# A linear-attention and mixture-of-experts kernel: loads one tile less ahead, two weight slices later, routing's matmuls and their readers issued apart

## The chip, the core and the metric

The kernel runs on one core of one Trainium2 chip. The metric is device time in microseconds of one execution, the median over several runs. Engines are named as the profile does: PE (TensorE, matmuls), DVE (VectorE), ACT (ScalarE), POOL (GpSimd), SP (SyncE, which here only issues DMAs).

## The reference

Two stages, the output of the first being the tokens of the second.

```python
for t in range(S):                       # B=4, H=8, S=768, D=48
    cur = einsum('bhd,bhe->bhde', u * k_t, v_t)
    y[:, :, t] = einsum('bhd,bhde->bhe', r_t, state + cur)
    state = w * state + einsum('bhd,bhe->bhde', k_t, v_t)
x = y as [3072 tokens, 384]
noisy = x @ w_gate + log1p(exp(x @ w_noise)) * noise     # 8 experts
top2 and their softmax weights per token
out[token] = sum over its 2 experts of weight * (relu(x @ w1[e]) @ w2[e])   # 384 -> 1024 -> 384
```

## The kernel before

**Attention** is done in 24 tiles of 128 rows (4 batches, 6 chunks; loop from L1224). Per tile: POOL forms kd (k times a table of decay, L391) and rku (r times k times u, L398 and L402); PE turns kd and r to head-major (KX and RV, L217); ACT and DVE evict them as kT and rT (L428, L430); PE forms the scores PAB (L443), DVE masks them as am (L451, two halves); PE forms py (L499), DVE adds the u term: x (L518), which SP stores to the DRAM tensor xd. Then PE turns x and multiplies it by the gate weights (L527), ACT copies the logits lg (L536). The work of neighbouring tiles overlaps: turn and scores of tile i+1 are issued in iteration i.

**Loads.** `load(i, part)` (L143) issues k, r and v of a tile on SP, in the row with everything else that SP issues: x stores, the noise nz, slices of expert 0's weights (stg, L338). In iteration i, k and r of tile i+6 and v of tile i+5 are issued; the prologue has loaded tiles 0 to 4 and k, r of 5. `W_LD` (L47) says in which iteration each of the seven weight slices is loaded, `W_AT0` (L48) from which iteration on its split into a high and a low part runs (ACT L344, L347, DVE L346, L349).

**Routing** runs beside attention, by groups of eight tiles (tiles 0 to 7, 8 to 15, 16 to 23). `route(g)` (L674) is a generator that issues one or two small DVE instructions between yields: the noisy logits, the two largest, softmax weights GTS, the count of earlier tokens per expert by matmuls into RT (L763 to L766, read by acc L767 and SLF L772), and the list of expert 0's rows. That list is made by `drop` (L627): one-hot tables r_oa and r_ob on DVE, then `place` (L653), which issues eight matmuls (L656) and in the same call DVE's reader of them (L660 or L662). `place` is put on the list `late_mm` and called two ticks later. In attention, `one_step` (L1131) advances a route by one yield, eight times per tile; `tick` (L1121) calls what is due in `late_mm`. In the expert stage `rstep` (L1159) does both, with a credit per call.

**Experts.** Each expert takes up to 832 rows, in chunks of tiles of 128: `p1(e, ci)` is the first matmul (ph L1044, evicted by ACT L1046 and DVE L1048 to hb), `p2(e, ci)` the second (pym L1078, 24 per tile of rows). Rows of a chunk come by a gather on POOL (xg, L947) that takes its indices from GR (DVE L810 to L812, after `place`), and PE turns them (ptm, L970). Expert 0's chunk 0 needs only group 0's tokens, its chunk 1 group 1's, and chunk 2 the rest. Gather and turn of chunk 1: `list_01` (L1197) gathers when group 1's `place` has run; the turn is issued at the fourth and fifth call of `step` in p2(0,0) (L1312), eight pym matmuls each. Chunk 2's are at the fourth to sixth call in p2(0,1) (L1346). While p1(0,0) runs, SP issues sixteen stores of zeros to the output (`zero_out`, L1212).

Of the kernel before, what the change touches and what calls it, by code (L numbers as in the profile page):

```python
# [43 lines left out]
W_AT = ((3, 7, 8), (3, 5, 7, 9))  # L44
NOT = 4

W_LD = {1: 0, 3: 1, 5: 2, 7: 3, 9: 4, 11: 5, 14: 6}  # L47
W_AT0 = (4, 6, 8, 11, 13, 16, 18)  # L48


@with_exitstack
def kernel(
# [574 lines left out]
    def drop(g, mm2, ej2, ijv, w_, c0, first):  # L627

        i0, i1 = GROUPS[g]
        n = i1 - i0  # L630
        wp_ = w_ + w_ % 2
        T = T_of(n)
        oa = T("oa", [128, n, 128], BF16, 2)
        ob = T("ob", [128, n, 2 * E * NJ], BF16, 2)[:, :, :2 * wp_].rearrange("p n (a b) -> p n a b", a=2)
        sh = [128, n, 64, 2]
        nc.vector.tensor_tensor(oa.rearrange("p n (a b) -> p n a b", b=2), mm2[:, :, None, :].to_broadcast(sh),  # L636
                                im[:, None].to_broadcast(sh), op=ALU.is_equal)
        yield 0.6
        c = 0.1 + 0.005 * wp_
        sh = [128, n, wp_ // 2, 2]  # L640
        o0, o1 = (ob[:, :, a].rearrange("p n (a b) -> p n a b", b=2) for a in range(2))
        nc.vector.tensor_tensor(o1, ej2[:, :, None, :].to_broadcast(sh),
                                ijv.rearrange("p (a b) -> p a b", b=2)[:, None].to_broadcast(sh), op=ALU.is_equal)
        yield c
        nc.vector.tensor_mul(o0, o1, thi[:, i0:i1, None, :].to_broadcast(sh))
        yield c
        late_mm.append([2, lambda: place(n, oa, ob, wp_, w_, c0, first),
                        lambda: nc.scalar.activation(ob[:, :, 1], ob[:, :, 1], AF.Copy, scale=pcol)])
        yield 0.05

    late_mm = []

    def place(n, oa, ob, wp_, w_, c0, first):  # L653
        pL = RT[:, 6 * GB * E:6 * GB * E + 2 * wp_].rearrange("p (a b) -> p a b", a=2)
        for j in range(n):
            nc.tensor.matmul(pL.rearrange("p a b -> p (a b)"), oa[:, j, :],  # L656
                             ob[:, j].rearrange("p a b -> p (a b)"), start=(j == 0), stop=(j == n - 1))
        Lv = L[:, :, c0:c0 + w_]
        if first:
            nc.vector.tensor_copy(Lv, pL[:, :, :w_])  # L660
        else:
            nc.vector.tensor_add(Lv, Lv, pL[:, :, :w_])  # L662
# [11 lines left out]
    def route(g, lists=True):  # L674
# [8 lines left out]
        if g:  # L683
            while lists and late_mm and g < len(GROUPS) - 1:
                yield "hold"
            pc = RT[:, 5 * GB * E:5 * GB * E + E]
            nc.tensor.matmul(pc, ones_b, acc, start=True, stop=True)
            sh0 = T("da", [128, n])[:, 0:1]
            nc.vector.tensor_scalar(sh0, pc[:, 0:1], -1.0, float(EARLY[g]), op0=ALU.mult, op1=ALU.add)
            yield  # L690
            nc.vector.tensor_max(ie_n[:, 0, 0:1], ie_n[:, 0, 0:1], sh0)
# [72 lines left out]
        for j in range(1, n):  # L764
            nc.tensor.matmul(pr[:, j:], ones_b, om[:, :n - j], start=False, stop=False, skip_group_check=True)
        nc.tensor.matmul(pr, ones_b, acc[:, None, :].to_broadcast(sh), start=False, stop=True, skip_group_check=True)  # L766
        nc.vector.tensor_add(acc, acc, sm[:, :, 0])  # L767
        next(ex, None)
        yield
# [351 lines left out]
    def tick():  # L1121
        for x in late_mm:
            x[0] -= 1
            if x[0] == 1:
                x[2]()
        while late_mm and late_mm[0][0] <= 0:
            late_mm.pop(0)[1]()
            credit[0] -= 0.25
        at_pe[0] = max(at_pe[0] - 1, 0)

    def one_step():  # L1131
        k = 0
        while len(route_q) > k and not at_pe[0]:
            try:
                c = next(route_q[k])
            except StopIteration:
                route_q.pop(k)
                continue
            if c == "wait" and k == 0 and FILL:
                k = 1  # L1140
                continue
            if c == "pe":
                at_pe[0] = 2
            return

    consts_a()
# [3 lines left out]
    uterm_u(0)  # L1150
    scores(0)
    mask(0)
    load(4)
    load(5, (0, 2))
    warm(WARM3)
    turn_kr(1)
    uterm_b(0)
# [1 line left out]
    def rstep(us, lag=2):  # L1159

        credit[0] = min(credit[0] + us, 1.6 * us + 0.2)
        for x in late_mm:
            x[0] -= 1
            if x[0] == 1:
                x[2]()
        while late_mm and late_mm[0][0] <= 0:
            late_mm.pop(0)[1]()
            credit[0] -= 0.25
        k = 0
        while len(route_q) > k:  # L1170
            if at_pe[0] > 0:
                at_pe[0] -= 1
                if at_pe[0] > 0:
                    return
            if credit[0] <= 0:
                return
            try:
                c = next(route_q[k])
            except StopIteration:
                route_q.pop(k)  # L1180
                continue
            if c == "wait" and k == 0 and FILL:
                k = 1
                continue
            if c in ("hold", "wait"):
                return
            if c == "pe":
                at_pe[0] = lag
                credit[0] -= 0.3
                return  # L1190
            credit[0] -= c or 0.25
# [31 lines left out]
    flag = consts_c()  # L1223
    for i in range(NT):  # L1224
        products(i)
        if i + 6 < NT:
            load(i + 6, (0, 2))
        if i == I_EARLY:
            while 0 not in routed or late_mm:
                rstep(1)  # L1230
            early(0)
        if i in (4, 6):
            next(flag)
        if 1 <= i <= B:
            load_nz(i - 1)
        if i == B:
            consts_b()
        if i:
            kvup(i)
        yout(i)  # L1240
        if not i:
            kvup(i)
        if i + 5 < NT:
            load(i + 5, (2, 3))
        zup_v(i)
        if i:
            zblock(i - 1)
            uterm_c(i, CV_EARLY, H)
            logits_out(i - 1)
            route_when_done(i - 1)  # L1250
        tick()
        one_step()
        one_step()
        if i + 1 < NT:
            uterm_b(i + 1)
        one_step()
        one_step()
        xout(i)
        one_step()
        if i == NT - 1:  # L1260
            xT_first()
            turn_x(i)
            p1a = p1(0, 0)
        else:
            turn_kr(i + 2)
            uterm_c(i + 1, 0, CV_EARLY)
            scores(i + 1)
            turn_x(i)
            mask(i + 1)
            tick()  # L1270
            one_step()
        if not i:
            consts_v()
        for p, t in enumerate(W_AT0):
            if W_LD.get(i) == p or t <= i <= t + 2:
                next(wun[p])
# [264 lines left out]
```

## Time and profile before

| | us |
|---|---|
| median of 3 runs (lowest, highest) | 591.69 (591.44, 592.29) |
| profiled execution | 594.2 |
| its span | 592.5 |
| attention, to the first matmul of p1(0,0) | 133.3 |
| p1(0,0), to the first pym of p2(0,0) | 143.12 |
| PE busy | 565.8 (96%) |
| DVE busy | 359.4 (61%) |
| ACT busy | 286.5 (48%) |
| POOL busy | 274.0 (46%) |

The shares are of the whole span. A window's row gives the busy time of each engine in a stretch, the number of instructions after an x, then the granted clock of PE as a share of full speed, the busy share of the DMA engines and GB/s. A row of waits says who waited for what: total, times, longest. In a timeline, the bracket at the end of a row is the idle time of its engine before it, and what ended it.

### The profile page before, as it was taken

How to read it: one execution, taken by the hardware profiler on the slowest of the kernel's cores; microseconds unless marked ns; L12 is line 12 of the kernel's file. 1: busy time of each engine (PE TensorE's matmuls, PEld its weight loads, DVE VectorE, ACT ScalarE, POOL GpSimd, SP SyncE). 2: the span in 40 equal slices, each digit the busy share in tenths (PEclk: the TensorE clock that was granted, in tenths of full speed). 3: DMA queues.
4: the chain of work that ended last, by engine and by line, in shares of the span. 5: the costliest groups of instructions: out<-in, count | busy, mean ns of one | idle time of the engine just before them, and what ended most of it. 6: DMA issues, size and time to landing. Idle time of an engine off the chain costs nothing.

```text
span 592.5 us, 13758 instructions
## 1 busy us (share of the span) xinstructions
PE 565.8 (96%) x5281; PEld 540.4 (91%) x5282; DVE 359.4 (61%) x866; ACT 286.5 (48%) x721; POOL 274.0 (46%) x420
## 2 busy tenths in 40 slices
PE   7897987889999999999999999999999999999995
PEld 5897886879999999999999999999999999999995
DVE  5998998977886554546455645555454546454331
ACT  4456786853362633554445554454545454445220
POOL 8987876721015543426333552344242526333222
PEclk9899999999999999999999999999999999999999
DMA  9989999429514643874655645464845555423211
GB/s 149 192 204 191 225 209 196 102 70 267 182 60 146 203 143 84 194 173 152 140 168 113 198 114 175 102 181 111 198 129 159 153 134 174 124 93 84 66 35 42
DMA packets 143016, 86.44 MB, mean 146 GB/s; under 512 B 118415, under 2 KB 133006, under 8 KB 142944
## 3 DMA queue, kind: packets, MB, share of 16 engines
q1 hardware_dynamic: 132384, 56.67, 40.6%
q0 software_dynamic: 9936, 28.83, 15.9%
q8 instruction: 43, 0.70, 0.5%
q14 instruction: 29, 0.24, 0.1%
q10 hardware_dynamic: 624, 0.00, 0.1%
HBM read 58.83 MB, written 19.76 MB: 133 GB/s over the span
## 4 chain that ended last, share of the span: by engine, by line
PE 79%; DVE 10%; DMA 5%; ACT 2%; POOL 2%; issue 2%; POOLq 0%; SPq 0%; ACTq 0%
PE ph L1044 35%; PE pym L1078 33%; PE py L499 2%; PE pym L1069 2%; PE pym L1071 2%; DVE am L451 2%; DMA stg<-in_moe_w_dram 2%; DVE x L518 2%; DVE rT L430 1%; DMA xg<-xd,GR 1%; DMA out_dram<-ot,TK 1%; PE KX L217 1%; DVE c L410 1%; PE py L527 1%; PE PAB L443 1%
## 5 line engine op out<-in xcount | busy, mean ns | idle before, releaser
L1078 PE MATMUL pym<-w1h,hb 128*128 128x384 f32 x768 | 200.6, 337 | 0.0
L1048 DVE SCALAR_TENSOR_TENSOR hb<-ph,hb 128x384 fp32r<-128x384 f32 (+1 forms) x136 | 72.5, 533 | 116.3 <-ACT ht L1046 68.4
L1044 PE MATMUL ph<-xh,w0h 128*128 128x384 f32 (+3 forms) x408 | 140.0, 344 | 0.0
L1078 PEld LDWEIGHTS pym<-w1h,hb 128*128 128x128 f32 x768 | 139.4, 188 | 0.3
L1044 PE MATMUL ph<-xh,w0l 128*128 128x384 f32 (+3 forms) x408 | 138.8, 341 | 0.0
L1044 PE MATMUL ph<-xl,w0h 128*128 128x384 f32 (+3 forms) x408 | 133.5, 341 | 0.0
L1078 PE MATMUL pym<-w1l,hb 128*128 128x384 f32 x384 | 129.5, 337 | 0.0
L1046 ACT ACTIVATE hb<-ph 128x384 fp32r<-128x384 f32 (+1 forms) x136 | 64.2, 472 | 107.7 <-PE ph L1044 105.0
L1101 POOL DMA_INDIRECT out_dram<-ot,TK x56 | 58.8, 1050 | 103.6 <-DVE ot L1097 52.6
L947 POOL DMA_INDIRECT xg<-xd,GR x56 | 61.2, 1092 | 70.6 <-DVE r_oa L636 18.8
L1044 PEld LDWEIGHTS ph<-xh,w0h 128*128 128x128 f32 x408 | 76.7, 188 | 3.3 <-ACT xh L987 0.2
L1044 PEld LDWEIGHTS ph<-xh,w0l 128*128 128x128 f32 x408 | 76.7, 188 | 2.6
L1044 PEld LDWEIGHTS ph<-xl,w0h 128*128 128x128 f32 x408 | 76.1, 188 | 2.8
L1078 PEld LDWEIGHTS pym<-w1l,hb 128*128 128x128 f32 x384 | 72.1, 188 | 0.1
L956 POOL DMA_INDIRECT pv<-out_dram,GA x49 | 49.8, 1016 | 48.2 <-DMA out_dram<-ot,TK 35.8
L1018 ACT ACTIVATE xh<-xj 128x384 fp32r<-128x384 f32 (+1 forms) x42 | 21.1, 502 | 43.5 <-DVE xj L1016 41.6
L1086 ACT ACTIVATE ot<-pym 128x384 f32<-128x384 f32 x39 | 19.0, 486 | 40.6 <-PE pym L1078 29.9
L1019 DVE TENSOR_TENSOR xl<-xj,xh 128x384 fp32r<-128x384 f32 (+1 forms) x42 | 22.4, 534 | 24.7 <-ACT xh L1018 13.6
L1004 ACT ACTIVATE pl<-xg 128x768 uint16<-128x768 uint16 (+1 forms) x42 | 35.3, 841 | 1.0 <-DMA xd<-pl 0.9
L391 POOL TENSOR_TENSOR kd<-kt,tabk 128x192 f32<-128x192 f32 x46 | 27.7, 624 | 12.8 <-PE RV L463 6.4
L451 DVE TENSOR_TENSOR am<-PAB,mneg 128x512 int32<-128x512 int32 x48 | 31.6, 680 | 1.9 <-PE PAB L443 1.8
L419 ACT ACTIVATE cv<-vt,c 128x48 f32<-128x48 f32 x120 | 30.2, 323 | 5.0 <-DVE c L410 2.6
(272 smaller groups left out, 827.3 us busy)
## 6 DMA issues: line engine op xcount, KB each, us to landing
stg<-in_moe_w_dram SPq DMA_DIRECT2D x24, 512.0 KB
stg<-in_moe_w_dram SPq DMA_DIRECT2D x32, 384.0 KB
rd<-in_r_dram SPq DMA_DIRECT2D x24, 192.0 KB
vt<-in_v_dram SPq DMA_DIRECT2D x24, 192.0 KB
xd<-x SPq DMA_DIRECT2D x24, 192.0 KB
out_dram<-ot SPq DMA_DIRECT2D x16, 288.0 KB
kt<-in_k_dram SPq DMA_DIRECT2D x23, 192.0 KB
xg<-xd,GR POOLq DMA_INDIRECT x56
```

Source lines behind the costliest of these rows:

```text
L391: nc.gpsimd.tensor_mul(KD[i][:, h], kt[i][:, h], tabk[:, h, :D])
L419: nc.scalar.activation(CV[i][:, h, :], vt[i][:, h, :], AF.Copy, scale=C8[i][:, h, :])
L451: nc.vector.tensor_tensor(am[:, :, h].bitcast(I32), pa[:, :, h].bitcast(I32), mneg[:, None].to_broadcast([128, 2, NP // 2, 128]), op=ALU.b ...
L947: nc.gpsimd.indirect_dma_start(out=xg[:n], out_offset=None, in_=xd[:rows_of(early_)], in_offset=bass.IndirectOffsetOnAxis(ap=GR[:n, e * NJ ...
L956: nc.gpsimd.indirect_dma_start(out=pv[:n], out_offset=None, in_=out, in_offset=bass.IndirectOffsetOnAxis(ap=GA[:n, e * NJ + t:e * NJ + t + ...
L1004: nc.scalar.activation(pl[:n], XG[e, t][:n, :DM].bitcast(U16).rearrange("p (d two) -> p two d", two=2), AF.Copy)
L1019: nc.vector.tensor_sub(xl, xj, xh.bitcast(F32))
L1044: nc.tensor.matmul(ph[:, :w_], a[:, d, fs], x[:, d, :w_], start=(j == 0), stop=(j == len(q) - 1))
L1046: nc.scalar.activation(h_[:, f, 0, :], ph[:, a:b], AF.Relu)
L1048: nc.vector.scalar_tensor_tensor(h_[:, f, 1, :], ph[:, a:b], 0.0, h_[:, f, 0, :].bitcast(F32), op0=ALU.max, op1=ALU.subtract)
L1078: nc.tensor.matmul(py, hb[:, f, a, hs], x[:, f, :], start=(j == 0), stop=(j == len(q) - 1))
L1101: st = nc.gpsimd.indirect_dma_start(out=out, out_offset=bass.IndirectOffsetOnAxis(ap=TK[:n, q:q + 1], axis=0), in_=ot[:n], in_offset=None, ...
```

## The change

Loads: the prologue leaves out v of tile 4 and k, r of tile 5; iteration i loads k and r of tile i+5 and v of tile i+4. Weight slices 5 and 6 are loaded in iterations 14 and 17 instead of 11 and 14, and the splits of slices 3 to 6 begin in iterations 10, 12, 17 and 20 instead of 11, 13, 16 and 18. `place` is split: the matmuls are issued at one tick and the reader (`placed`) at the next one. In `route`, two yields stand between a matmul and its reader. One `one_step` call less stands in each tile.

```diff
-W_LD = {1: 0, 3: 1, 5: 2, 7: 3, 9: 4, 11: 5, 14: 6}
-W_AT0 = (4, 6, 8, 11, 13, 16, 18)
+W_LD = {1: 0, 3: 1, 5: 2, 7: 3, 9: 4, 14: 5, 17: 6}
+W_AT0 = (4, 6, 8, 10, 12, 17, 20)
...
-        late_mm.append([2, lambda: place(n, oa, ob, wp_, w_, c0, first),
-                        lambda: nc.scalar.activation(ob[:, :, 1], ob[:, :, 1], AF.Copy, scale=pcol)])
+        pL = RT[:, 6 * GB * E:6 * GB * E + 2 * wp_].rearrange("p (a b) -> p a b", a=2)
+        late_mm.append([2, lambda: place(n, oa, ob, pL),
+                        lambda: nc.scalar.activation(ob[:, :, 1], ob[:, :, 1], AF.Copy, scale=pcol),
+                        lambda: placed(pL, w_, c0, first), False])
...
-    def place(n, oa, ob, wp_, w_, c0, first):
-        pL = RT[:, 6 * GB * E:6 * GB * E + 2 * wp_].rearrange("p (a b) -> p a b", a=2)
+    def place(n, oa, ob, pL):
...
+
+    def placed(pL, w_, c0, first):
...
             nc.tensor.matmul(pc, ones_b, acc, start=True, stop=True)
+            yield "pe1"
...
         nc.tensor.matmul(pr, ones_b, acc[:, None, :].to_broadcast(sh), start=False, stop=True, skip_group_check=True)
+        yield "pe1"
         nc.vector.tensor_add(acc, acc, sm[:, :, 0])
...
-        while late_mm and late_mm[0][0] <= 0:
-            late_mm.pop(0)[1]()
-            credit[0] -= 0.25
+        if late_mm and late_mm[0][4]:
+            late_mm.pop(0)[3]()
+        if late_mm and late_mm[0][0] <= 0:
+            late_mm[0][1]()
+            late_mm[0][4] = True
...
-            if c == "pe":
-                at_pe[0] = 2
+            if c in ("pe", "pe1"):
+                at_pe[0] = 2 if c == "pe" else 1
...
-    load(4)
-    load(5, (0, 2))
+    load(4, (0, 2))
...
         while late_mm and late_mm[0][0] <= 0:
-            late_mm.pop(0)[1]()
+            x = late_mm.pop(0)
+            if not x[4]:
+                x[1]()
+            x[3]()
             credit[0] -= 0.25
...
+            if c == "pe1":
+                continue
...
-        if i + 6 < NT:
-            load(i + 6, (0, 2))
+        if i + 5 < NT:
+            load(i + 5, (0, 2))
...
-        if i + 5 < NT:
-            load(i + 5, (2, 3))
+        if i + 4 < NT:
+            load(i + 4, (2, 3))
...
         one_step()
         if i + 1 < NT:
             uterm_b(i + 1)
-        one_step()
         one_step()
```

Three places show how it moves the instructions. The first is DVE in attention around the reader acc of group 0's counting matmuls (zt is the state update, c the u term's sum, r_sm the counts, w1l the low part of a weight slice). Before:

```order
L410 TENSOR_REDUCE c_1811<-rku 128x8
L518 TENSOR_TENSOR x<-py,cv 128x384
L430 TENSOR_TENSOR rT<-RV,pwr 128x2x4x64
L451 TENSOR_TENSOR am<-PAB,mneg 128x2x256 x2
L349 TENSOR_TENSOR w1l_1129<-stg,w1h_1128 128x384
L476 TENSOR_TENSOR zt<-RV,z_210 128x192
L767 TENSOR_TENSOR acc<-acc,r_sm 128x8
L558 TENSOR_SCALAR RT<-r2r 128x8
L772 TENSOR_TENSOR SLF_239<-RT,ie_n 128x64
L561 SCALAR_TENSOR_TENSOR RT<-RT,r2r 128x8
L410 TENSOR_REDUCE c_1936<-rku 128x8
```

And now:

```order
L476 TENSOR_TENSOR zt<-RV,z_210 128x192
L410 TENSOR_REDUCE c_1927<-rku 128x8
L518 TENSOR_TENSOR x<-py,cv 128x384
L430 TENSOR_TENSOR rT<-RV,pwr 128x2x4x64
L451 TENSOR_TENSOR am<-PAB,mneg 128x2x256 x2
L772 TENSOR_TENSOR acc<-acc,r_sm 128x8
L558 TENSOR_SCALAR RT<-r2r 128x8
L349 TENSOR_TENSOR w1l_1124<-stg,w1h_1123 128x384
L476 TENSOR_TENSOR zt<-RV,z_211 128x192
L777 TENSOR_TENSOR SLF_239<-RT,ie_n 128x64
L561 SCALAR_TENSOR_TENSOR RT<-RT,r2r 128x8 x2
L410 TENSOR_REDUCE c_2045<-rku 128x8
```

The matmuls that acc reads stand on PE after its py of the same tile. The reader stood behind the state update zt of its tile; now the x addition, the rT eviction and both masks of the next tile stand between, and SLF comes two more instructions later. L767 has become L772, L772 is L777.

The second is DVE at the rows GR of expert 0's chunk 1, from which the gather of p2(0,0) takes its indices (hb is the eviction of p1, PS the route of group 2, xl<-ptm the reader of the turned rows). Before, the reader of ptm stood 22 rows further down:

```order
L693 SCALAR_TENSOR_TENSOR PS<-lg 128x64
L695 TENSOR_SCALAR r_a<-PS 128x64
L696 SCALAR_TENSOR_TENSOR PS<-lg,nz 128x64
L549 TENSOR_SCALAR PS<-r_a 128x64
L1048 SCALAR_TENSOR_TENSOR hb<-ph,hb 128x256
L662 TENSOR_TENSOR L<-L,RT 128x2x7
L810 SCALAR_TENSOR_TENSOR lt<-L 128x2
L811 TENSOR_SCALAR lt<-lt 128x2
L812 TENSOR_SCALAR GR<-lt 128x2
L1048 SCALAR_TENSOR_TENSOR hb<-ph,hb 128x256
L551 TENSOR_SCALAR PS<-PS 128x64
```

And now:

```order
L558 TENSOR_SCALAR PS<-r1r 128x64
L561 SCALAR_TENSOR_TENSOR PS<-PS,r1r 128x64 x2
L665 TENSOR_TENSOR L<-L,RT 128x2x7
L815 SCALAR_TENSOR_TENSOR lt<-L 128x2
L816 TENSOR_SCALAR lt<-lt 128x2
L817 TENSOR_SCALAR GR<-lt 128x2
L561 SCALAR_TENSOR_TENSOR PS<-PS,r1r 128x64 x2
L977 TENSOR_TENSOR xl<-ptm,xh 128x3x128
L561 SCALAR_TENSOR_TENSOR PS<-PS,r1r 128x64
L563 SCALAR_TENSOR_TENSOR PS<-PS,r1s 128x64
```

GR is computed within p2(0,0), after all of p1(0,0)'s evictions, and the reader of ptm is two rows behind it. On PE, the eight matmuls of `place` (L657) stand behind 24 pym of p2(0,0), and ptm 8 pym behind them; before, they stood in p1(0,0) and 32 pym of p2(0,0) lay between p1's end and ptm. In p2(0,1) it is the same with 16 pym before `place` and 16 behind it; there `place` stood ahead of the first pym.

The third is SP at the end of attention (r_a are the gate weights of a group that are stored beside x, out_dram<-ot the zero stores). Before:

```order
L520 DMA xd<-x 128x384
L152 DMA vt<-in_v_dram 128x8x48
L520 DMA xd<-x 128x384 x6
L793 DMA xd<-r_a 128x8x8
L1213 DMA out_dram<-ot 192x1x384 x16
L793 DMA xd<-r_a 128x8x8
L338 DMA stg<-in_moe_w_dram 128x1024 x3
```

And now:

```order
L152 DMA vt<-in_v_dram 128x8x48
L520 DMA xd<-x 128x384
L152 DMA vt<-in_v_dram 128x8x48
L520 DMA xd<-x 128x384 x5
L1224 DMA out_dram<-ot 192x1x384 x10
L798 DMA xd<-r_a 128x8x8
L1224 DMA out_dram<-ot 192x1x384 x6
L798 DMA xd<-r_a 128x8x8
```

Group 1's gate weights, which the gather of chunk 1 reads with the rows, stand behind ten of the zero stores; before, ahead of all.

## Rows read from the trace of the kernel before

**Rows 1.** The page, busy us (share of the span) and instructions.

```profile
PE 565.8 (96%) x5281; PEld 540.4 (91%) x5282; DVE 359.4 (61%) x866; ACT 286.5 (48%) x721; POOL 274.0 (46%) x420
```

**Rows 2.** Windows of 10 us (us, busy of each engine, PEclk, DMA, GB/s).

```profile
100.00:110.00 10.00, 7.82 (x191) 7.13 (x192) 9.65 (x31) 6.93 (x22) 5.79 (x12) 1.00 0.92 198
140.00:150.00 10.00, 10.00 (x74) 9.92 (x74) 8.41 (x40) 2.73 (x8) 1.93 (x2) 1.00 0.95 296
```

**Rows 3.** Window, the tiles from x9 to x23.

```profile
58.13:132.29 74.16, 62.27 (x1521) 57.25 (x1523) 68.00 (x205) 53.98 (x185) 50.13 (x87) 0.98 0.71 163
```

**Rows 4.** Waits of DVE, 50 to 134 us.

```profile
DVE acc L767 <- PE RT L766: 2.8, 2, 2.2
...
DVE L L660 <- PE RT L656: 1.4, 1, 1.4
```

**Rows 5.** Timeline of DVE, first and last of group 1's moved part.

```profile
120.67 0.16 DVE L747 TENSOR_SCALAR r_da<-r_da 128x8 f32<-128x8 f32 x1
...
132.77 0.21 DVE L792 TENSOR_TENSOR r_a<-r_os 128x64 f32<-128x64 f32 x1
```

**Rows 6.** Timeline of PE, tile 22: py of the masked scores.

```profile
126.06 1.09 PE L499 MATMUL py<-vt,am 128*64 128x48 f32 x32
```

**Rows 7.** Timeline of DVE: acc of group 1, x22.

```profile
127.52 0.17 DVE L767 TENSOR_TENSOR acc<-acc,r_sm 128x8 bf16<-128x8 bf16 x1 [2.24 <-PE RT L766]
...
128.89 0.55 DVE L518 TENSOR_TENSOR x<-py,cv 128x384 f32<-128x384 f32 x1
```

**Rows 8.** Waits of ACT (25:80) and POOL (10:80) for loads.

```profile
ACT w0h L344 <- DMA stg<-in_moe_w_dram: 4.6, 2, 3.0
...
POOL kd L391 <- DMA kt<-in_k_dram: 5.2, 5, 1.8
```

**Rows 9.** Timeline of SP: weight slice 2.

```profile
50.63 1.42 SPq L338 DMA_DIRECT2D stg<-in_moe_w_dram  x1
```

**Rows 10.** Windows, all engines, around the idle PE at 56 us.

```profile
55.97:58.80 2.83, 0.00 (x0) 0.00 (x0) 1.38 (x8) 2.79 (x12) 2.14 (x5) 0.93 1.23 226
58.80:61.80 3.00, 2.91 (x46) 2.75 (x48) 3.00 (x8) 2.70 (x10) 2.60 (x6) 0.50 0.83 188
```

**Rows 11.** Timeline of PE: p2(0,0) start, ptm; p2(0,1) start, place.

```profile
143.12 0.34 PE L1078 MATMUL pym<-w1h,hb 128*128 128x384 f32 x1
...
148.76 0.49 PE L970 MATMUL ptm<-ident,xg 128*128 128x128 f32 x3
...
161.33 0.42 PE L1078 MATMUL pym<-w1h,hb 128*128 128x384 f32 x1
...
165.65 0.53 PE L656 MATMUL RT<-r_ob,r_oa 128*128 128x100 bf16 x8
```

**Rows 12.** Timeline of DVE: GR of chunk 1; chunk 2.

```profile
142.27 0.17 DVE L812 TENSOR_SCALAR GR<-lt 128x2 int32<-128x2 f32 x1
...
161.79 0.42 DVE L1048 SCALAR_TENSOR_TENSOR hb<-ph,hb 128x256 fp32r<-128x256 f32 x1
162.12 0.16 DVE L662 TENSOR_TENSOR L<-L,RT 128x14 f32<-128x14 f32 x1
...
162.72 0.17 DVE L812 TENSOR_SCALAR GR<-lt 128x3 int32<-128x3 f32 x1
162.79 0.68 DVE L636 TENSOR_TENSOR r_oa<-r_dm,im 128x1024 bf16<-128x1024 bf16 x1
```

**Rows 13.** Timeline of POOL: gathers of chunk 1 and of chunk 2.

```profile
142.71 0.98 POOL L947 DMA_INDIRECT xg<-xd,GR  x1 [15.77 <-DVE GR L812]
144.00 0.95 POOL L947 DMA_INDIRECT xg<-xd,GR  x1 [0.30 <-issue]
163.74 0.95 POOL L947 DMA_INDIRECT xg<-xd,GR  x1 [18.79 <-DVE r_oa L636]
```

**Rows 14.** DMA, gathers' queue: 142.5 to 146.0, 163.5 to 166.5.

```profile
q0 software_dynamic: 64, 0.20, 26.0%
...
q0 software_dynamic: 64, 0.20, 26.3%
```

## The prediction

> **What bounds the kernel now.** I read the page's engine totals first, then windows, then the waits of one engine at a time. The totals [rows 1] say that TensorE (PE) is busy for 96% of the span and VectorE (DVE) for 61%, but that is an average over two stages. The windows separate them [rows 2]: from 140 us on PE is busy 10.0 of 10 us at full clock, so the expert stage costs what PE has to do, and anything PE waits for there is added whole. In the attention stage it is the other way round: from 100 to 110 us DVE is busy 9.65 of 10 and PE 7.82. So in attention a DVE instruction or a DVE stall that goes is worth its time, until another engine's chain ends later; in the expert stage small DVE instructions are free. I cut the attention loop at the starts of its x additions, one per tile: from the tenth to the last tile (x9 to x23) it is 74.16 us, of which DVE works 68.00 and is idle 6.16 [rows 3].
>
> Times of the sum are those of the profiled execution (594.2 us, span 592.5). The median of the runs shown is 591.69; I add the differences to the median, since what the sum changes is a difference. A difference of 0.2% (1.2 us) is about what a measurement of this kernel can tell from none.
>
> **Readers issued apart, and eight steps per tile to seven.** The waits of DVE [rows 4] are what the split removes: 2.8 us before acc L767, which reads RT behind nine matmuls, and 1.4 before L660, which reads place's matmuls. The order shows in place of these waits a mask (am) or another tile's work between matmul and reader. The step that is missing per tile makes routing later: the part of group 1 from L747 to L792, 23 small instructions of 0.16 to 0.29 us, leaves the attention loop and is done in the expert stage's first p1. The first and the last are in [rows 5]; together they are 4.05 us. If DVE alone set the end, 4.05 + 2.8 + 1.4 = 8.25 us would go. It does not quite, and I go through the places:
> - Eight of the 23 stand before acc, in tiles where DVE has nothing idle: 1.43 us, all gained.
> - Tile 22, where 2.24 of the acc wait is: x22 starts at 128.89 [rows 7]. Without acc before it, it still needs PE's py, which ends at 126.06 + 1.09 = 127.15 [rows 6]. So 1.74 goes, not 2.24 and the instructions behind it.
> - The other acc wait, 2.8 - 2.24 = 0.6, and L660's 1.4: both gained, 2.0.
> - Of tile 23, behind x22, I take 0.4 for the instructions that leave it, since PE's chain there is hardly shorter than DVE's, and 0.2 for L792 [rows 5], which stands ahead of the first expert's xl.
> That is 1.43 + 1.74 + 2.0 + 0.4 + 0.2 = **5.8 us** gained, with ends 3.5 (x22 and x23 wait for ACT or PE just as long) and 8.25. What the moved instructions cost in the expert stage is nothing by themselves: in 140 to 150 us DVE is busy 8.41 of 10 [rows 2], and PE waits for none of it but what the next part says.
>
> **Loads one tile later, weights 5 and 6 later.** SyncE's queue issues transfer after transfer in the attention loop, each waiting its turn, so a transfer's place in the row decides when it starts. With one k/r/v triple less ahead of it, each slice of weights starts earlier. Slice 2 was issued at 50.63 [rows 9] and ACT waited 2.98 us for it, to 55.52; over both slices 4.6 us [rows 8]. With it comes an idle PE from 55.97 to 58.80 with the clock at 0.50 in the 3.0 us behind it [rows 10]. So a gain of up to the length of that idle time, 2.8 us, is there. Against it, POOL already waits 5.2 us in five places for k [rows 8], and k of tile n is now issued one iteration later, behind one more x store and in part one more slice: k itself comes some 1.5 us later, and POOL's product kd is ahead of the turn and scores of the next tile. So one wait is exchanged for another in the same tiles. I take **0.6 us** gained, ends 2.8 gained and 2.5 lost (half of the 5.2 again). Slices 5 and 6 have their splits in tiles 17 to 22 instead of 16 to 20; they are needed in the first p2 alone (143 us), so nothing waits. The DVE halves of the split are the same count.
>
> The Trainium skill (DMA: Bandwidth & Descriptors, Rules for kernel authors) speaks against this part: to overlap transfer and work, issue the DMA early and wait late. By that rule the 0.6 gained would be the 2.5 lost. The trace does not show it settled, since the row of transfers is full either way: what is issued early there is late for another.
>
> **The first two gathers of the expert stage.** This is the part that costs. Group 1's place matmuls now stand inside p2(0,0), behind 24 of its pym matmuls, where they stood in p1(0,0), before. Call T the start of p2(0,0); it was 143.12, and the first turn ptm came at 148.76 = T + 5.64, 32 matmuls of 0.176 us later [rows 11]. Before, the rows GR were computed at 142.27 [rows 12], ahead of T, the gather ran from 142.71 [rows 13], its 64 packets were done by 146.0 [rows 14], and PE waited for nothing. Now: 24 matmuls x 0.176 = T + 4.2, place 0.3, then L665 and L815 to L817, 0.8 us as from 162.12 to the end of GR at 162.89 [rows 12]: T + 5.35. The gather starts 0.3 us behind GR's end: T + 5.6. It lands 3.3 us later under the zero stores (142.71 to 146.0), 2.8 without them (163.74 to 166.5) [rows 13, 14]: T + 8.4 to 8.9. PE is at ptm at T + 5.64 + 0.25 for the added matmuls, T + 5.9. PE's wait is **2.8 us**, ends 2.3 and 4.1 (the chunk's second gather, issued 1.3 us behind the first [rows 13], is waited for whole).
>
> In p2(0,1) the same happens to group 2. PE reaches its first ptm 32 pym and eight place matmuls (0.35) after the start, T2 + 5.9 ([rows 11] has T2 = 161.33 and the place at 165.65). DVE has a chain of twelve instructions, two of them r_oa of 0.68 us [rows 12], the others 0.16 to 0.2, after the last hb of p1(0,1), which ended at 161.79 + 0.42, T2 + 0.9: then T2 + 4.3, GR at T2 + 5.0, gather T2 + 5.3, landed T2 + 8.1. PE waits **2.2 us**, ends 1.0 and 2.75. The gathers of the third chunk have a whole p1 more and are not waited for.
>
> Behind an idle time of 2.83 us PE's granted clock was 0.50 for 3.0 us [rows 10], the 1.2 GHz level. Of two waits of 2.8 and 2.2 us I let one be followed by that: 3.0 x 0.5 = **1.5 us**, ends 0 and 3.0.
>
> **Sum:** -5.8 - 0.6 + 2.8 + 2.2 + 1.5 = +0.1. Rounded to what this bears, 591.5 us: no change, with a gain in attention paid back in the first two p2.
>
> **The rivals.**
> 1. *The weights come in time and no wait for k takes their place* (chance 0.24). The idle PE at 56 us is gone, its whole 2.83 us with it. For it: the longest single wait of that stretch is the one for a slice. Against: five k waits. With 2.8 in place of 0.6, and no clock fall in p2: 591.5 - 2.2 - 1.5 = 587.8.
> 2. *Loads issued later are late* (0.16). Place: POOL's kd in tiles 5 to 12. It decides if k of a tile lands more than about 1 us later than now, for there the turn of the tile has no slack. 2.5 lost in place of 0.6 gained: 591.5 + 3.1 = 594.6, slower. It is the case that the rule in the Trainium skill (DMA: Bandwidth & Descriptors, Rules for kernel authors) would bring.
> 3. *More waiting in the expert stage* (0.10): the second gather of the chunk is waited for too, with the upper ends 4.1 and 2.75, and both clock falls: 591.5 + 1.3 + 0.55 + 1.5 = 594.9, slower.
> 4. *The gathers are covered after all* (0.08), because DVE and the gather are quicker than I price them: without 2.8 + 2.2 + 1.5 the time is 585.0. The order speaks against it: in DVE's row the reader of ptm stands two rows behind GR.
>
> **How the numbers follow.** My forecast has 0.42, its own range 589.8 to 593.2: 0.08 of it over 1.2 us faster, 0.28 within, 0.06 slower. Faster: 0.08 + 0.22 of rival 1 + 0.08 of rival 4 = 0.38. Same: 0.28 + 0.02 of rival 1 = 0.30. Slower: 0.06 + 0.16 + 0.10 = 0.32. For 8 in 10 the range takes in rivals 1 and 2 and most of 3, and leaves 4 out: 587.0 to 595.4.
>
> **What would show it.** In the profile after, DVE should have no wait for RT at acc L772 and L663 and x9 to x23 should be some 68 us; expert work should start near 127 us instead of 133.3. The ACT wait for stg should be under 1 us, POOL's for kt should be 5 us or more. PE should be idle 2 to 4.5 us before the first ptm of p2(0,0) and 1 to 2.75 before that of p2(0,1), released by the DMA xg, with a granted clock of 0.50 behind at least one. If PE is idle in neither, the main costs are wrong and the time is rival 4's; if the expert stage starts later than 130 us, the attention gain is wrong.

## The result, and the profile after

The changed kernel takes 600.57 us (median of 4 runs, 598.14 to 602.03) against 591.99 us (591.44 to 594.12). The ratio over all the runs is 1.0134, with a 95% interval of 1.0086 to 1.0182; the quotient of the two medians is 1.0145. It is slower, outside the range of the prediction. The ratios of this document leave out executions more than 1.5% above the fastest of their kernel, which are three of e10's five (606.7 to 609.5 us, the traced one among them). Its profiled execution, the shortest of the four, took 598.14 us with a span of 596.4. Rows below are of that execution; their differences to the rows of before therefore add up to 3.9 us, not to the 8.6 between the medians.

The attention loop did what was expected, and more. One window, from x9 to x23 as in [rows 3]:

```profile
57.00:123.99 66.99, 59.89 (x1512) 55.81 (x1514) 64.49 (x186) 53.94 (x184) 50.02 (x87) 1.00 0.79 178
```

74.16 us have become 66.99, and p1(0,0) starts at 125.03 in place of 133.33. DVE works 64.49 us in place of 68.00. The waits of DVE (50 to 134 us, the largest three), to be held against [rows 4], and the waits of POOL for k (10 to 80 us), against [rows 8]:

```profile
DVE hb L1053 <- ACT hb L1051: 2.9, 3, 1.6
DVE x L518 <- ACT lg L536: 1.0, 2, 0.8
DVE zt L476 <- PE RV L463: 0.3, 1, 0.3
```

```profile
POOL kd L391 <- DMA kt<-in_k_dram: 7.9, 7, 2.5
```

No wait for RT is left on DVE. ACT has no wait for a weight slice there; POOL waits 7.9 us for k where it waited 5.2.

All of it and more is paid back in the expert stage. The timeline of PE at the start of p2(0,0), at its `place` matmuls, at its first ptm, and at the start and the first ptm of p2(0,1), against [rows 11]:

```profile
134.75 0.34 PE L1083 MATMUL pym<-w1h,hb 128*128 128x384 f32 x1
...
139.10 0.36 PE L657 MATMUL RT<-r_ob,r_oa 128*128 128x16 bf16 x8
...
144.64 0.90 PE L975 MATMUL ptm<-ident,xg 128*128 128x128 f32 x3 [3.67 <-DMA xg<-xd,GR]
...
158.58 0.34 PE L1083 MATMUL pym<-w1h,hb 128*128 128x384 f32 x1
...
167.83 0.60 PE L975 MATMUL ptm<-ident,xg 128*128 128x128 f32 x3 [3.15 <-DMA xg<-xd,GR]
```

Two idle times of 3.67 and 3.15 us, each ended by the DMA of a gather. Behind both the granted clock falls to the 1.2 GHz level; two windows of PE's work from the end of each idle time (the number before DMA share and GB/s is the clock):

```profile
144.64:148.10 3.46, 3.46 (x15) 3.42 (x15) 1.86 (x6) 0.58 (x2) 0.00 (x0) 0.57 0.09 36
167.83:171.30 3.47, 3.47 (x19) 3.42 (x20) 1.95 (x7) 1.10 (x3) 0.29 (x1) 0.54 0.21 71
```

A mean of 0.57 and 0.54 over 3.5 us: in both places nearly the whole stretch is at half clock, as in [rows 10]. Summed over half-microsecond windows, 3.4 us are lost to the clock, 0.2 of them while PE is still idle.

Why the first gather is so late is seen on DVE, POOL and SP. DVE from the writing of r_a over the instruction that waits to GR, and GR of chunk 2; POOL's gathers; SP's zero stores (the first two answer to [rows 12] and [rows 13]):

```profile
134.16 0.23 DVE L797 TENSOR_TENSOR r_a<-r_os 128x64 f32<-128x64 f32 x1
...
138.25 0.20 DVE L699 TENSOR_SCALAR r_a<-PS 128x64 f32<-128x64 f32 x1 [0.92 <-DMA xd<-r_a]
...
140.23 0.16 DVE L665 TENSOR_TENSOR L<-L,RT 128x14 f32<-128x14 f32 x1
...
140.82 0.17 DVE L817 TENSOR_SCALAR GR<-lt 128x2 int32<-128x2 f32 x1
...
163.53 0.17 DVE L817 TENSOR_SCALAR GR<-lt 128x3 int32<-128x3 f32 x1
```

```profile
141.26 0.98 POOL L952 DMA_INDIRECT xg<-xd,GR  x1 [22.00 <-DVE PS L561]
142.55 0.95 POOL L952 DMA_INDIRECT xg<-xd,GR  x1 [0.30 <-issue]
164.55 1.11 POOL L952 DMA_INDIRECT xg<-xd,GR  x1 [21.06 <-DVE r_ob L645]
```

```profile
124.96 8.91 SPq L1224 DMA_DIRECT2D out_dram<-ot  x10
134.41 0.49 SPq L798 DMA_DIRECT2D xd<-r_a  x1
134.95 5.69 SPq L1224 DMA_DIRECT2D out_dram<-ot  x6
```

The store of group 1's r_a stands behind ten zero stores in SP's row, but what it waited for is r_a itself: L797 ended at 134.39, and SP issued the store at 134.41. It landed 3.7 us later, where the two other stores of r_a in this execution took 2.4 and 2.9 us. So r_a was still being read when group 2's route wanted to write the tile again: DVE waits 0.92 us at L699, and L665, three rows of DVE ahead of GR, has to wait with it. What L665 reads, the `place` matmuls, had ended at 139.46, and L665 starts at 140.23; without the wait for r_a it could have started at most 0.8 us earlier. The gather starts at 141.26, T + 6.5 with T = 134.75, and PE gets on at T + 9.9.

The same stretches in all the executions traced, in us. The first column of times ends at the start of x9, the second goes from x9 to x23, and the ratio is the one to before on the same chip, with its 95% interval; the rows from e1 on are the experiments below.

| kernel | to x9 | x9 to x23 | p2(0,0) | p2(0,1) | p1 and p2(0,2) | ratio |
|---|---|---|---|---|---|---|
| before | 58.1 | 74.2 | 9.1 | 11.0 | 24.9 | 1 |
| the change | 57.0 | 67.0 | 14.8 | 16.1 | 26.7 | 1.0134 (1.0086 to 1.0182) |
| again (e9) | 60.7 | 67.4 | 15.5 | 16.1 | 28.5 | 1.0105 (1.0069 to 1.0140) |
| again (e15) | 59.9 | 67.5 | 15.4 | 14.6 | 26.8 | 1.0096 (1.0058 to 1.0134) |
| e1, loads and weights alone | 58.9 | 72.3 | 9.1 | 11.0 | 24.9 | 0.9971 (0.9950 to 0.9993) |
| e12, k, r, v alone | 60.0 | 74.3 | 9.1 | 11.0 | 24.7 | 1.0001 (0.9982 to 1.0019) |
| e13, weights alone | 57.7 | 73.2 | 9.1 | 11.0 | 24.3 | 0.9981 (0.9962 to 1.0000) |
| e2, split alone, eight steps | 59.8 | 68.9 | 14.6 | 13.8 | 26.9 | 1.0079 (1.0048 to 1.0111) |
| e11, seven steps alone | 58.3 | 70.7 | 12.6 | 15.3 | 26.6 | 1.0130 (1.0098 to 1.0161) |
| e4, change with eight steps | 59.0 | 68.8 | 14.6 | 13.7 | 26.3 | 1.0083 (1.0053 to 1.0113) |
| e7, change with ten steps | 59.8 | 74.2 | 9.3 | 11.0 | 24.8 | 0.9987 (0.9963 to 1.0011) |
| e5, change, routing early in p1 | 60.4 | 67.3 | 14.4 | 12.8 | 24.5 | 1.0122 (1.0090 to 1.0153) |
| e6, change, known rows at tile 21 | 58.4 | 70.9 | 9.6 | 12.4 | 26.3 | 1.0018 (0.9998 to 1.0038) |
| e14, change, known rows in p1 | 60.5 | 68.1 | 9.6 | 12.4 | 27.0 | 0.9973 (0.9953 to 0.9993) |
| e8, change with zeros in the waits | 57.9 | 67.1 | 13.5 | 14.5 | 26.3 | 1.0073 (1.0044 to 1.0102) |
| e10, change, zero stores early | 57.7 | 67.0 | 14.0 | 16.1 | 25.9 | 1.0096 (1.0052 to 1.0140) |

The stretch from x9 to x23 is nearly the same in four executions of one loop (67.0, 67.4, 67.5 of the change and 67.1 of e8), while the one to x9 lies between 57.0 and 60.7: POOL waits 5.6 to 7.0 us for k up to 60 us in these four, and what else sets that length is not shown. The two p2 vary too, 14.6 to 16.1 for the second, with whether the clock falls. So the clean columns are x9 to x23 and the p2, and the ratios. p1(0,0) and p1(0,1) have no column: they took 9.7 to 9.9 and 8.9 to 9.3 us, but 12.0 and 13.3 in e5, 15.95 for the first in e10, and 10.7 (e6) and 10.0 (e14) for the second.

### The profile page after: what moved, and what is told of

The parts are those of the page before. It is cut to its first block, busy times and chain, and to the rows that moved or that the text cites. A ratio compares the mean times of both kernels' runs of the same rounds, so it can differ in the third digit from the quotient of the medians.

```text
span 596.4 us, 13757 instructions
## 1 busy us (share of the span) xinstructions
PE 566.4 (95%) x5281; PEld 540.5 (91%) x5282; DVE 358.5 (60%) x866; ACT 286.9 (48%) x721; POOL 274.8 (46%) x420
## 4 chain that ended last, share of the span: by engine, by line
PE 76%; DVE 10%; DMA 7%; POOL 2%; issue 2%; SPq 2%; ACT 1%; POOLq 0%; DVEq 0%
PE ph L1049 36%; PE pym L1083 31%; DMA kt<-in_k_dram 3%; DVE am L451 2%; PE pym L1074 2%; PE pym L1076 2%; PE py L499 2%; SPq L152 1%; DMA vt<-in_v_dram 1%; DVE rT L430 1%; DMA xg<-xd,GR 1%; DVE x L518 1%; DMA out_dram<-ot,TK 1%; PE PAB L443 1%; PE ptm L975 1%
## 5 line engine op out<-in xcount | busy, mean ns | idle before, releaser
L1053 DVE SCALAR_TENSOR_TENSOR hb<-ph,hb 128x384 fp32r<-128x384 f32 (+1 forms) x136 | 72.3, 532 | 116.8 <-ACT ht L1051 73.2
L1083 PEld LDWEIGHTS pym<-w1h,hb 128*128 128x128 f32 x768 | 141.0, 190 | 0.2
L1106 POOL DMA_INDIRECT out_dram<-ot,TK x56 | 58.9, 1052 | 99.0 <-DVE ot L1102 51.5
L961 POOL DMA_INDIRECT pv<-out_dram,GA x49 | 51.4, 1049 | 49.1 <-DMA out_dram<-ot,TK 36.7
L1024 DVE TENSOR_TENSOR xl<-xj,xh 128x384 fp32r<-128x384 f32 (+1 forms) x42 | 22.5, 535 | 24.7 <-ACT xh L1023 24.7
```

The source lines that it names most:

```text
L961: nc.gpsimd.indirect_dma_start(out=pv[:n], out_offset=None, in_=out, in_offset=bass.IndirectOffsetOnAxis(ap=GA[:n, e * NJ + t:e * NJ + t + ...
L1024: nc.vector.tensor_sub(xl, xj, xh.bitcast(F32))
L1053: nc.vector.scalar_tensor_tensor(h_[:, f, 1, :], ph[:, a:b], 0.0, h_[:, f, 0, :].bitcast(F32), op0=ALU.max, op1=ALU.subtract)
L1083: nc.tensor.matmul(py, hb[:, f, a, hs], x[:, f, :], start=(j == 0), stop=(j == len(q) - 1))
L1106: st = nc.gpsimd.indirect_dma_start(out=out, out_offset=bass.IndirectOffsetOnAxis(ap=TK[:n, q:q + 1], axis=0), in_=ot[:n], in_offset=None, ...
```

## The experiments

**Theory G**, after the result: routing work put off makes the gathers of expert 0's second and third chunk late, PE waits for them and works at half clock behind. Rivals: **L**, the loads one tile later cost; **S**, the routing work moved into the expert stage holds DVE, hb comes late, and PE waits for that; **R**, the split of the readers costs by itself. The experiments ran on several chips, on which before took 594.5 to 596.8 us, not 592; where an expectation names times in us, they are to be read by the ratio.

**The parts, one at a time: e1, e2, e4.** e1 is before with this and no more:

```diff
-W_LD = {1: 0, 3: 1, 5: 2, 7: 3, 9: 4, 11: 5, 14: 6}
-W_AT0 = (4, 6, 8, 11, 13, 16, 18)
+W_LD = {1: 0, 3: 1, 5: 2, 7: 3, 9: 4, 14: 5, 17: 6}
+W_AT0 = (4, 6, 8, 10, 12, 17, 20)
-    load(4)
-    load(5, (0, 2))
+    load(4, (0, 2))
-        if i + 6 < NT:
-            load(i + 6, (0, 2))
+        if i + 5 < NT:
+            load(i + 5, (0, 2))
-        if i + 5 < NT:
-            load(i + 5, (2, 3))
+        if i + 4 < NT:
+            load(i + 4, (2, 3))
```

> Before, with the loads and weight slices of the change alone (readers and eight steps as before; place of groups 1 and 2 stays ahead of p2). Theory G (the loss is PE's idle time at the two gathers plus the half clock behind, the attention part gains): no idle PE at ptm, attention 0 to 3 us shorter, 589 to 592. Rival L (loads issued one tile later are what costs): 594 or more, with POOL's wait for kt up from 5.2 us to 7.9 as in the change.

Measured: 0.9971 (594.25 us against 595.97), x9 to x23 1.8 us shorter, no idle PE at a ptm of p2(0,0) or p2(0,1). Rival L falls, though it had named 594 or more: before took 595.97 there, and POOL waited 5.8 us for k, not 7.9. The loads and weights are the one part that gains.

e2 is the change with those lines as before, and with the eighth step back:

```diff
         if i + 1 < NT:
             uterm_b(i + 1)
+        one_step()
         one_step()
```

> The change without its loads and weights and with eight steps per tile: only the readers are issued apart. Routing still falls behind far enough that place of group 1 stands behind 16 pym of p2(0,0), and of group 2 behind 16 of p2(0,1). Theory G: attention some 4 us shorter, PE idle about 2.3 us at the first ptm (8 pym less than in the change, 3.67 there) and about 3 at the second, half clock behind both: 594 to 599. Rival L: near 588, as the loads are as before.

Measured: 1.0079, with idle PE of 3.35 and 2.43 us at the two ptm. The split alone puts routing off far enough, since each added yield uses up a step (one yield is new at each of two places in `route`, and `place` and its reader are now a tick apart).

e4 is the change with the same eighth step.

> The change with eight steps per tile. Place of group 1 stands behind 16 pym of p2(0,0) in place of 24, of group 2 as in the change. Theory G: the first idle time falls by about 1.4 us to 2.3, the second stays at 3.1; attention 1 to 3 us longer than in the change: 597 to 601, no better than the change. Rival S (it is the routing work moved into the expert stage that holds DVE and so PE, not the gathers): fewer moved instructions, so 2 or 3 us faster than the change.

Measured: 1.0083, idle PE 3.28 and 2.38 us. The first idle time fell by less than I expected and the second fell too; attention was 1.8 us longer from x9 to x23 than in the change. The ratio is 0.1 to 0.5% below the three of the change, and the intervals overlap: this run doesn't part G from S. The execution traced was the longest of its four (603.78 us). It lost some 5 us more in expert 1's first p1, which took 18.4 us in place of 13.2, with PE idle for 3.3 us until an hb and at half clock behind; the traces of the change have nothing like it, and its cause is not shown.

**Routing earlier in p1: e5.**

```diff
-STEPS_P1 = 0.8
+STEPS_P1 = 1.6
```

> The change with the routing credit per p1 block raised from 0.8 to 1.6 (one constant): more routing work in p1(0,0) and p1(0,1), so that both place stand ahead of the p2 again and 32 pym lie between p2(0,0)'s start and ptm; the attention loop is that of the change, word for word. Theory G: no idle PE at either ptm, no half clock there, attention 8.3 us shorter: 583 to 586. Rival S: DVE is held in p1 by the added routing work, hb comes late, PE waits in p1 instead: 592 or more. Rival L: still over 592.

Measured: 1.0122. Theory G's numbers were wrong here, and rival S has a part in it. In the order, place stands ahead of p2(0,0); in time it does not help: DVE comes to its reader L665 at 143.84, behind group 2's rows, two hb and the wait for r_a. Window of p1(0,0); then DVE's two rows and PE's first ptm in the timelines:

```profile
128.67:140.68 12.01, 10.36 (x102) 9.87 (x103) 8.26 (x41) 3.94 (x13) 0.00 (x0) 1.00 0.82 241
```

```profile
141.32 0.20 DVE L699 TENSOR_SCALAR r_a<-PS 128x64 f32<-128x64 f32 x1 [0.87 <-DMA xd<-r_a]
...
144.43 0.17 DVE L817 TENSOR_SCALAR GR<-lt 128x2 int32<-128x2 f32 x1
```

```profile
149.69 0.55 PE L975 MATMUL ptm<-ident,xg 128*128 128x128 f32 x3 [3.12 <-DMA xg<-xd,GR]
```

p1(0,0) takes 12.01 us in place of 9.7, PE is busy 10.36 of it, and GR still comes 3.8 us after p2(0,0) has begun (140.68). PE now waits in its own row for routing: 0.75 and 0.90 us ahead of routing matmuls in p1(0,0), and 3.0 us ahead of `place` matmuls in p1(0,1), which took 13.27 us in place of 9.05. So pushing the routing work into p1 did not bring the rows in time, and cost PE time there; an order of DVE's row with GR further ahead was not tried.

**The waits taken away: e6 and e14.** Both let the gathers of chunks 1 and 2 take the rows of chunk 0, which are known since tile 21; those two chunks are computed from rows that are not theirs. e6 issues chunk 1's gathers in tile 21, e14 in p1(0,0):

```diff
-                in_offset=bass.IndirectOffsetOnAxis(ap=GR[:n, e * NJ + t:e * NJ + t + 1], axis=0))
+                in_offset=bass.IndirectOffsetOnAxis(ap=GR[:n, col:col + 1], axis=0))
...
-        early(1)
+        rows(EARLY[1] // 128, EARLY[2] // 128, rows_of(1))
...
+    xgather(0, 1, 0, (0, 1))
     for j, _ in enumerate(p1a):
...
-        xgather(0, 2)
...
+    xgather(0, 2, 0, (0, 1, 0))
     route_q.extend([list_0(), rest(0), rest(1), rest(2), list_1()])
```

> The change, but the gathers of expert 0's chunks 1 and 2 take their rows from the indices of chunk 0, which are known since tile 21, and are issued at tile 21 and at the start of p1(0,1): nothing waits for them. This leaves out the right rows for those two chunks (their tokens are computed from other rows); all routing instructions, place and the turns stand where they stand in the change. Theory G (PE's loss is the wait for the gathers and the half clock behind): no idle PE at the two ptm, p2(0,0) 9.2 us in place of 14.8 and p2(0,1) 11 to 12 in place of 16, so 9 to 11 us faster than the change, ratio to before 0.990 to 0.996. Rival S (routing work in the expert stage holds DVE and so PE): the two p2 stay over 12 us, ratio over 1.003.

Measured: 1.0018. The idle times at ptm are gone, and p2(0,0) is 9.6 us. But tile 22 took 8.03 us, and the waits of PE (120 to 215 us) say why; the gathers that I had put there hold it, as e14 bears out, where they stand elsewhere and tile 22 takes 5.15 us again:

```profile
PE py L527 <- ACT xT L437: 3.2, 1, 3.2
PE RT L657 <- DVE L L663: 1.1, 1, 1.1
```

So this run mixed a cost of its own with the one removed, and e14 was made without it, with the changed kernel beside it (e15):

> As e6_known_rows (the gathers of chunks 1 and 2 of expert 0 take the rows of chunk 0, so those two chunks are computed from other rows than the reference's), but chunk 1's gathers are issued at the start of p1(0,0), behind the attention loop, so that they can't hold tile 22 as they did there (8.03 us in place of 5.15). Theory G: attention as long as in the change, no idle PE at the two ptm, full clock behind them: some 3 us faster than e6_known_rows, ratio 0.993 to 0.999, so that the whole loss of the change is in the waits for the gathers and what follows them. If the ratio stays at 1.002 or more, a part of the loss is elsewhere.

> The changed kernel on the same chip, as the base for the run beside it: ratio 1.008 to 1.016, p2(0,0) 14.5 to 15.5 us and p2(0,1) 16 us long.

Measured: e14 0.9973, e15 1.0096. Without the waits, and with nothing else of the change undone, the loss is gone: the two ratios differ by 1.2% of 597 us, 7.3 us. p2(0,0) is 9.55 us long in place of 15.37, p2(0,1) 12.41 in place of 14.60. The windows of the two, e14's first, then e15's first ptm in the timeline of PE:

```profile
139.47:149.02 9.55, 9.55 (x65) 9.16 (x64) 6.72 (x34) 2.48 (x7) 0.91 (x1) 1.00 0.93 267
159.02:171.43 12.41, 10.91 (x83) 10.06 (x82) 10.06 (x39) 5.56 (x14) 0.00 (x0) 1.00 0.41 129
```

```profile
148.44 0.55 PE L975 MATMUL ptm<-ident,xg 128*128 128x128 f32 x3 [4.06 <-DMA xg<-xd,GR]
```

So the loss against before goes with the waits, which is theory G. Rival S is not nothing, though: p2(0,0) is still 0.4 us longer than before, p1(0,1) 0.9, p2(0,1) 1.4, where PE waits 1.1 us for DVE's L663, and the third chunk 2.1. Together that is 4.9 of the 6.0 us that x9 to x23 gained in e14.

**The clock: e8 and e9.** Zeros are multiplied in the two waits, into the tile that ptm then overwrites:

```diff
             pt = psm[0].tile([128, ND, 128], F32, name="ptm", tag="pt", bufs=2)
+            if e == 0 and t in (2, 4):
+                for _ in range(18):
+                    nc.tensor.matmul(pt, wsrc, wsrc[:, None, :].to_broadcast([128, ND, 128]), start=True, stop=True)
```

> The change with 18 matmuls of zeros (wsrc) into ptm ahead of its turns, once in p2(0,0) and once in p2(0,1), where PE is idle for 3.67 and 3.15 us: about 3 us of PE work in the wait. Theory G with the clock as a part of the loss: granted clock 1.00 behind both waits in place of 0.50, and 3 to 4 us faster than the change (ratio about 1.006). If the clock costs nothing, the ratio stays at that of the change.

> The changed kernel again, on the chip of the other three, so that they can be compared with it: 1.009 to 1.018 of before, PE idle 3 to 4 us before the first ptm and about 3 before that of p2(0,1), half clock behind both.

Measured: 599.37 us against 602.97 for the changed kernel, ratios 1.0073 and 1.0105. Windows of e8 behind the two waits:

```profile
144.50:148.00 3.50, 2.72 (x19) 2.36 (x17) 1.18 (x5) 0.65 (x3) 0.17 (x1) 1.00 0.31 93
168.00:172.00 4.00, 4.00 (x37) 3.77 (x34) 3.03 (x11) 1.68 (x5) 0.00 (x0) 1.00 0.19 54
```

Full clock in both, and no half clock anywhere from 120 to 220 us. That is 3.6 us by the medians and 1.9 by the ratios, and the intervals of the two ratios overlap. So the size rests on the traces: 3.4 us in the first execution of the change; 5.1 in e9, where the clock fell at a third place too, in p2(0,2); 1.7 in e15, where it fell once. The execution of e8 that was traced lost 2.6 us in expert 1's first p1 (15.8 us in place of 13.2), as e4's did.

**The other pieces: e7, e10, e11, e12, e13.** e7 is the change with ten steps per tile, so that group 1's place and count are where they were:

> The change with ten routing steps per tile in place of seven, which makes up for the steps that the added yields use: counting of group 1 is back in tile 22 and place stands where it stood before (32 pym ahead of the first ptm, place of group 2 ahead of p2(0,1)). Theory G: no idle PE at the ptm, p2(0,0) 9.1 us and p2(0,1) 11 us; attention shorter than before by the waits of DVE that are gone and by the loads, 2 to 5 us: ratio 0.991 to 0.997. Rival L: no better than the loads alone, 0.997, or worse. If attention is as long as before, the split itself brings nothing and the gain of the change in attention was the work it put off.

Measured: 0.9987, no idle PE at a ptm, x9 to x23 74.2 us. The last sentence of the expectation holds: with all routing work in attention the split and the loads leave the loop as long as it was, though no reader waits for RT any more. Its clock there had a mean of 0.95 where before had 0.98, so a part may be PE's:

```profile
59.82:134.03 74.21, 63.88 (x1523) 59.36 (x1523) 67.51 (x201) 53.26 (x183) 48.69 (x85) 0.95 0.71 156
```

e11 is before with one `one_step` call less per tile:

> Before with seven routing steps per tile in place of eight and nothing else: the readers stand right behind their matmuls, loads as before. Place of groups 1 and 2 stands behind 16 pym of the two p2. Theory G: attention 2 to 4 us shorter than before by the work put off, two idle times of 2 to 3.5 us with half clock behind: ratio 1.004 to 1.010, as with the split at eight steps (1.0079). Rival R (the split itself is what costs): 1.00 or less.

Measured: 1.0130, above the 1.004 to 1.010 expected and as slow as the whole change, with 2.85 and 2.33 us idle at the two ptm. Rival R falls as the cause of the loss: no reader was moved, and one step less per tile does it.

e12 and e13 part the loads from the weights (the weights are the four lines at the head of e1's diff).

> Before with k, r and v loaded one tile later and nothing else. Loads and weights together gave 0.9971. If it is the shorter row ahead of the slices that helps: 0.995 to 0.999. If the later slices 5 and 6 are the gain: 1.000 or a little more.

> Before with weight slices 5 and 6 and the splits moved as in the change and nothing else. If the shorter row of k, r and v is the gain of the loads: 0.999 to 1.001 here. If the later slices are: 0.996 to 0.999.

Measured: 1.0001 and 0.9981. The distance of k, r and v is worth nothing that can be told; the later slices are the likelier source of e1's gain, though the upper end of e13's interval is 1.0000. What they gain lies in the tiles from 14 on: 5.45 us in place of 5.90 from x13 to x14, 4.70 in place of 5.17 from x17 to x18.

e10 issues the zero stores in tiles 19 to 22, four each:

```diff
+        if i in (19, 20, 21, 22):
+            for j in range(4):
+                zero_out((i - 19) * 4 + j)
...
-    for j, _ in enumerate(p1a):
-        zero_out(2 * j)
-        zero_out(2 * j + 1)
+    for _ in p1a:
         rstep(STEPS_P1)
-    zero_out(14)
-    zero_out(15)
```

> The change with the sixteen zero stores issued in tiles 19 to 22, four each, where the DMA engines are little used, in place of during p1(0,0). Group 1's gate weights are then no longer behind ten of them in SP's row. Theory G: DVE's wait for the store of r_a (0.92 us at L699 in the change) goes and the gather of chunk 1 lands in 2.8 us in place of 3.4, so the first idle time falls from 3.7 or 4.2 to some 2.3; attention as long as in the change; 1 to 2.5 us faster than the change, ratio 1.006 to 1.012. If neither changes, the gather is late by DVE's row alone.

Measured: 1.0096, which cannot be told from the change's 1.0096 to 1.0134. The ratio rests on two executions (597.25 and 603.17 us), and the one traced is not among them, so its rows say nothing of the ratio. In it the x stores were behind the zero stores, and ACT's first eviction of p1(0,0) waited for one. ACT's row and PE's first ptm in the timelines:

```profile
132.13 0.38 ACT L1051 ACTIVATE hb<-ph 128x256 fp32r<-128x256 f32 x1 [5.86 <-DMA xd<-x]
```

```profile
150.55 0.68 PE L975 MATMUL ptm<-ident,xg 128*128 128x128 f32 x3 [2.68 <-DMA xg<-xd,GR]
```

The first idle time was 2.68 us, GR started 5.35 us after p2(0,0) in place of 6.07, and DVE had no wait for r_a. But L699 came 4.1 us after L797, as late as it came in the change with its wait, since the held p1(0,0) had slowed DVE's row too. So this run does not show what the zero stores cost; the rows of the change bound the wait for r_a at 0.8 us of the first idle time.

## Why the prediction was wrong, by its own steps

The step that failed is the price of the expert stage. The forecast had 2.8 + 2.2 + 1.5 = 6.5 us for the two waits and the clock, and nothing for work that is put off. In the profiled execution p2(0,0) and p2(0,1) took 10.7 us more and the third chunk 1.9, together 12.6, and the attention gain, 8.3 in place of 6.4, makes up for 1.9 of the difference. The mechanism was right: the signs listed came true or nearly so, but for the second wait, which at 3.15 us was over its 2.75. By term:

- **Readers and steps, 5.8 us gained.** The size held: x9 to x23 lost 7.2 us, of which the loads and weights make up 1.8 (e1), and 5.4 are left. From x23 to the expert stage it is 1.04 us in both. The profiled execution also came to x9 1.1 us earlier. What I did not see is what the gain is made of. e7 shows that the split leaves the stretch at 74.2, even with the loads, when no work is put off; e11 shows that a missing step shortens it by 3.4. Removing a wait on DVE was worth little, as far as these runs can tell; leaving work for later was worth what the work costs, and that is taken back. The prediction put the moved instructions at nothing in the expert stage; in e14, even without the waits for the gathers, p1(0,1) to p2(0,2) are 4.5 us longer than before.
- **Loads, 0.6 us gained, ends 2.8 and -2.5.** e1 gives 1.7 us by its ratio (0.0029 x 596), within the ends. The reason was wrong. The wait of ACT for a slice [rows 8] did go: it is 4.6 to 4.8 us in before, e2 and e11, and none of the twelve executions traced that load k, r and v later has it. But e12 shows that this is worth nothing that can be told, and e13, whose loads are those of before as far as tile 9, had no such wait either. POOL's wait for k tells no more: 7.9 us in e2 with the loads of before, 3.0 in e12. The rule of the Trainium skill (DMA: Bandwidth & Descriptors, Rules for kernel authors) that spoke for a loss of 2.5 is not borne out either: k, r and v issued one tile later made 1.0001.
- **The first two gathers, 2.8 and 2.2 us.** The place and the mechanism were right, the sizes were not: 3.67 and 3.15 us in this execution, 4.1 to 4.2 and 3.2 in the two others. For the first, I had the four rows to GR start when place ends, and DVE's wait for the store of r_a (0.92) was not in the sum, though the order shows that store behind the zero stores; GR's row started at T + 6.07 in place of T + 5.2. For the second I let the gather start 0.3 us after GR's end, as chunk 1's did; it started 0.85 us after that end and 1.02 after GR's start (163.53 to 164.55), which [rows 12] and [rows 13] already showed for chunk 2 (162.72 to 163.74). Both then landed 3.3 to 3.4 us after their start, not 2.8.
- **Half clock once, 1.5 us.** It fell behind both waits: 3.4 us, in one execution 5.1 and in one 1.7. e8 keeps the clock up and is faster by 3.6 us by the medians, 1.9 by the ratios.
- **Not in the sum at all:** p1 and p2(0,2) took 1.9 us longer (3.7 in e9). In p1(0,2) it is one more group of place matmuls; in p2(0,2) PE waited 0.34 us for a gather and 1.04 for ACT's ot.

For the profiled execution: -8.3 to the expert stage, -0.1 in p1(0,0), +5.7 in p2(0,0), +5.1 in p2(0,1), +1.9 in the third chunk, -0.4 behind it, is +3.9, against the +0.1 of the sum. By the medians it is 8.6. Of the 4.7 between, 2.2 are that before's profiled execution was above its median (594.2 to 591.99), and 2.4 that the change's was below its own. The other runs of the change had mean clocks of 0.988, 0.989 and 0.986 where the profiled one had 0.993, and e9's and e15's executions took 60.7 and 59.9 us to x9 where this one took 57.0. Both are of that size; how it divides between them in the runs without a trace stays open.

Rival 3 had the right sign, place and nearly its upper ends, with a chance of 0.10; its price, 594.9, left out the third chunk.

**A version that beats both kernels** is e1, the loads and weights alone: 0.9971 (0.9950 to 0.9993), with nothing left out. That is 1.7 us, and the interval ends close to 1.

## What to carry to other kernels

Work taken out of a busy stage is not gained unless nothing in the next stage waits for its result: follow each put-off instruction to the transfer that needs it, and compare the arrival with the reader's place in time, not in the order. Where the next stage is bound by PE, a wait of 3 us there cost up to 5 here (3.15 and 1.7), because the clock fell behind it. A wait of one engine that another engine's chain would fill anyway (the readers of RT) is not a gain when it goes, as e7 suggests.

## What the runs showed of the hardware that was not expected

The clock did not follow the length of the idle time alone. In e11 it fell behind 2.33 us of idle PE and not behind 2.85; in e15 it did not fall behind 3.23; in e9 it fell behind idle times of 0.54 and 1.09. PE's windows from the end of these idle times, e11's two, then e15's second:

```profile
148.83:152.30 3.47, 3.47 (x22) 3.44 (x23) 2.23 (x9) 1.16 (x4) 0.00 (x0) 1.00 0.35 133
170.08:173.60 3.52, 3.52 (x23) 3.35 (x24) 1.95 (x7) 1.10 (x3) 0.35 (x1) 0.70 0.26 74
```

```profile
171.74:175.20 3.46, 3.46 (x33) 3.40 (x34) 2.17 (x8) 1.68 (x5) 0.20 (x1) 1.00 0.26 67
```

And e9's timeline of PE with its window:

```profile
201.79 0.52 PE L975 MATMUL ptm<-ident,xg 128*128 128x128 f32 x3 [0.54 <-DMA xg<-xd,GR]
203.41 0.44 PE L1074 MATMUL pym<-w1h,ht 128*128 128x384 f32 x1 [1.09 <-ACT ot L1089]
```

```profile
204.00:207.50 3.50, 3.50 (x14) 2.98 (x12) 0.80 (x2) 0.81 (x3) 2.66 (x4) 0.54 0.36 130
```

Each fall cost about 1.7 us. One to three of them in the expert stage of one program is a spread of 3.4 us, of the size of that of the change's runs (598.14 to 602.03).
